# One product in wider superblocks: 1024 and 512 tokens in place of 768, with pairs of weight sets in step

## The chip, the cores and the metric

The kernel runs on one core of a Trainium2 chip. Measured is the device time of one execution in microseconds (us); the median of three runs of the kernel before is 1436.38 us (1436.04 to 1436.53). A core has five engines that run side by side, each in its own order: TensorE (PE; its weight loads stand as PEld), VectorE (DVE), ScalarE (ACT), GpSimd (POOL) and SyncE (SP). DMAs are issued by SP, ACT and POOL and move data between the memory of the chip (HBM) and the core's SBUF. TensorE writes its results into PSUM, eight banks of 512 float32 per partition, which VectorE and ScalarE read.

## The reference

```python
scores = scale * q @ k.T                       # 8 batches, 8 heads, 576 tokens, 64 wide
x = ((scores * Dmat) @ v)                      # decay gamma ** (i - j) for i >= j, as (4608, 512)
h = (x @ w1) * (x @ w2) @ w3                   # 512 -> 1024 -> 1024
x = h @ w_out                                  # (4608, 512)
h = x @ w_in                                   # moe2: 512 -> 2048
g = h * np.clip(h + 3.0, 0.0, 6.0) / 6.0
out = g @ w_out2                               # 2048 -> 512
```

All in float32. The change is about `h = x @ w_in` and what makes g of it.

## The kernel before

Four stages follow each other on TensorE: the weights w3 @ w_out (start to about 60 us), attention and the first expert layer by blocks of 512 tokens (to 730.69 us, line 704), the first product of moe2 (to 1081.57, lines 895 to 924), and its second product (to the end, line 993). Precise products are made of three matmuls, high x high, high x low and low x high (`mm3`, lines 124 to 128), on operands of the type float32r.

The first product of moe2 works on 2 x 2 blocks by a scheme with seven products in place of eight (Strassen's, in Winograd's form). The weights stand in eight *sets* (`wset`), each with seven 256 x 128 combinations; the tokens in *superblocks* with seven *operands* (`xop`), each a combination of token halves and of halves of the 512 inputs, high and low part. A superblock of the kernel before has 2 x 384 = 768 tokens, and there are six. For each superblock and each set, `run_set` (line 771) makes seven products; each is 2 halves (`kk`) x 3 = 6 matmuls of 384 columns, in the order of the operands 0 to 6. They go to four banks: A takes products 0 and 3, B product 1, D products 2 and 5, C products 4 and 6. After product 0 ScalarE copies A into u; U = u + B and V = U + D are made by VectorE; the results are A after product 3, c22 = V + C, c12 = U + D and c21 = U + C after the last accumulation. The seventh product of a set comes after the first one of the next set (`pending`).

Each result goes through `gate` (line 743): ScalarE makes relu(r / 6 + 1/2), VectorE min(that, 1) times the result, and POOL issues the store to `gd` in HBM. Results wait for their store in tiles of `g_tile` (line 736): six of 384 columns and four more in two staging tiles `gw`, in turn. A tile is written again only when its store has landed. In the first set of the first superblock the relu's output takes such a tile as well.

The order of the work is written out by hand: `at(s, f)` puts f before the s-th call of `tick`, and each `mm3` makes one tick. That sets the order on each engine; when an instruction runs is decided by its semaphores. Operands are stored to HBM (`xod`) by the blocks of the stage before (`x2_store`, line 616) and loaded by SP (`load_xop`, line 680) into a ring of eleven places of 1536 columns; at the end of a superblock three places are free beyond the seven in use, and loads of the next operands start as places come free. Sets of weights are loaded once, from 706 us on (`load_set`, line 667); set 3 and later ones at the start of the stage. In the last superblock the places of weights that are done take the operands of the second product (`q_tile`, `q_late`).

Of the kernel before, what the change touches and what calls it, by code (L numbers as in the profile page):

```python
# [26 lines left out]
def retention_moe_kernel(  # L27
# [37 lines left out]
    BLK = 384  # L65
# [3 lines left out]
    NSB = NT // (2 * BLK)  # L69
    NSET = M2 // 2  # L70
    NX = 11
# [8 lines left out]
    xod = dram_p.tile([NSB, 7, 128, 2, 2, BLK], F32, name="xod")  # L80
# [234 lines left out]
    with tc.manual_schedule():  # L315
# [300 lines left out]
        def x2_store(j, kk):  # L616
            c = HB1 * j
            while c < HB1 * j + HB1:
                sb, a = divmod(c, BLK)
                n = min(BLK - a, HB1 * j + HB1 - c)  # L620
                for hl, t in enumerate((x2b["hi"], x2b["lo"])):
                    (nc.sync if j == NB - 1 else nc.scalar).dma_start(
                        out=xod[sb, :, :, kk, hl, a:a + n].rearrange("o p n -> p o n"),
                        in_=t[:, 0:7 * HB1].rearrange("p (o n) -> p o n", o=7)[:, :, c - HB1 * j:c - HB1 * j + n])
                c += n
# [41 lines left out]
        def load_set(n, pool, tag):  # L667
            wset[n] = w = pool.tile([128, 2, 7 * 256], F32R, tag=tag, name="wset")
            if n == 2:
                nc.scalar.copy(out=w[:, 0, 0:1], in_=half)  # L670
            elif n < 2:
                nc.gpsimd.memset(w.bitcast(F32)[:, 0, 0:1], 0.0)
            nc.sync.dma_start(out=w.bitcast(F32), in_=wid[n].rearrange("h p n -> p h n"))

        def ring(q, shape, dtype, name):
            k = q % NX
            pool = xo_p if 5 <= k < 7 else ap["xr" if k < 5 else "xl"]
            return pool.tile(shape, dtype, tag={5: "xh", 6: "xl"}.get(k, f"x{k}"), name=name)

        def load_xop(sb, i):  # L680
            xop[sb, i] = x = ring(7 * sb + i, [128, 2, 2, BLK], F32R, "xop")
            if sb == 0:
                nc.gpsimd.memset(x.bitcast(F32)[:, 0, 0, 0:1], 0.0)
            nc.sync.dma_start(out=x.bitcast(F32), in_=xod[sb, OPS[i]])
# [13 lines left out]
        for i, s in enumerate((20, 26, 32, 38, 44, 4, 52)):  # L698
            at(E0 + s, lambda i=i: load_xop(0, i))
# [14 lines left out]
        g_p = ctx.enter_context(tc.tile_pool(name="gp", bufs=6))  # L714
# [7 lines left out]
        tmp = [x[:, BLK * i:BLK * i + BLK] for x in (stg, stg_hi) for i in range(4)]  # L722
        t_at = {"u": (7,), "U": (5, 6), "V": (4, 3), "r": (0, 1, 2)}
# [9 lines left out]
        g_more = [wf_p.tile([128, 1024], F32, tag="wr", name="gw") for _ in range(2)]  # L733
        g_n = [0]

        def g_tile():
            g_n[0] += 1
            i, k = divmod(g_n[0] % 10 - 6, 2)
            if i < 0 or not g_more:
                return g_p.tile([128, BLK], F32, tag="g", name="g")  # L740
            return g_more[i][:, BLK * k:BLK * k + BLK]

        def gate(src, sb, m, h, keep=True):
            c = {}

            def f0():
                c["r"] = g_tile() if (sb, m % NSET) == (0, 0) else temp("r")
                nc.scalar.activation(out=c["r"], in_=src(), func=ACTF.Relu, bias=half, scale=1.0 / 6.0)

            def f1():  # L750
                c["g"] = src() if keep else g_tile()
# [3 lines left out]
            def f2():  # L755
                p0 = (2 * sb + h) * BLK
                nc.gpsimd.dma_start(out=gd[:, m, p0:p0 + BLK], in_=c["g"])

            for d, f in ((0, f0), (3, f1), (6, f2)):
                at(now[0] + d, f)  # L760

        def prod(sb, n, i, o, ps_, first, stop):
            w, x = wset[n], xop[sb, i]
            for kk in range(2):
                cs = slice(o * 256 + kk * 128, o * 256 + kk * 128 + 128)
                mm3(ps_[:, 0:BLK], w[:, 0, cs], w[:, 1, cs], x[:, kk, 0], x[:, kk, 1], first and kk == 0, stop and kk == 1, skip_group_check=True)
# [4 lines left out]
        def run_set(sb, n):  # L771
            c = {}

            def bank(k):
                c[k] = ps_bank()

            def u_copy():
                c["u"] = temp("u")
                nc.scalar.copy(out=c["u"], in_=c["A"][:, 0:BLK])

            def u2():
                c["U"] = temp("U")
                add(c["U"], c["u"], c["B"][:, 0:BLK])

            def v():
                c["V"] = temp("V")
                add(c["V"], c["U"], c["D"][:, 0:BLK])

            def c_of(k, a, b):
                def f():  # L790
                    c[k] = g_tile()
                    add(c[k], c[a], c[b][:, 0:BLK])
                return f

            bank("A")
            prod(sb, n, 0, 1, c["A"], True, True)
            at(now[0], u_copy)
            if pending:
                pending.pop()()
            bank("B")  # L800
            prod(sb, n, 1, 4, c["B"], True, True)
            at(now[0], u2)
            bank("D")
            prod(sb, n, 2, 3, c["D"], True, True)
            at(now[0], v)
            prod(sb, n, 3, 2, c["A"], False, True)
            gate(lambda: c["A"][:, 0:BLK], sb, n, 0, keep=False)
            bank("C")
# [252 lines left out]
```

## Time and profile before

| | |
|---|---|
| median of 3 runs | 1436.38 us |
| profiled execution | 1436.19 us |
| its span, from the first to the last instruction | 1434.4 us |
| busy: TensorE, weight loads, VectorE, ScalarE, GpSimd | 1428.4, 1241.8, 1019.0, 582.4, 153.1 us |
| first product of moe2 | 730.69 to 1081.57 us |
| HBM read and written | 175.94 and 109.58 MB |

The profiled execution's own time is its span and 1.8 us around it. Busy time of a matmul is modelled, and two that follow each other overlap, so what a matmul costs is read from the starts of its neighbours. The idle time of an engine that isn't the bottleneck costs nothing by itself. In the rows, "<-" behind an instruction stands between what it writes and what it reads; in brackets stands what ended the idle time before it.

### The profile page before, as it was taken

How to read it: one execution, taken by the hardware profiler on the slowest of the kernel's cores; microseconds unless marked ns; L12 is line 12 of the kernel's file. 1: busy time of each engine (PE TensorE's matmuls, PEld its weight loads, DVE VectorE, ACT ScalarE, POOL GpSimd, SP SyncE). 2: the span in 40 equal slices, each digit the busy share in tenths (PEclk: the TensorE clock that was granted, in tenths of full speed). 3: DMA queues.
4: the chain of work that ended last, by engine and by line, in shares of the span. 5: the costliest groups of instructions: out<-in, count | busy, mean ns of one | idle time of the engine just before them, and what ended most of it. 6: DMA issues, size and time to landing. Idle time of an engine off the chain costs nothing.

```text
span 1434.4 us, 27310 instructions
## 1 busy us (share of the span) xinstructions
PE 1428.4 (100%) x11144; PEld 1241.8 (87%) x11144; DVE 1019.0 (71%) x1751; ACT 582.4 (41%) x894; POOL 153.1 (11%) x283
## 2 busy tenths in 40 slices
PE   9999999999999999999999999999999999999999
PEld 4588888888888888888899999999999888888888
DVE  7897566665666656573556666666678889988997
ACT  6583334333434334343333333333344443343343
POOL 1101000000000000000012333223320000000000
PEclk9999999999999999999999999999999999999999
DMA  9843646464656555555799563645699444455541
GB/s 359 310 147 109 224 160 223 143 241 141 211 172 192 191 182 198 170 183 159 274 342 392 231 254 115 265 173 201 220 387 308 133 122 123 138 147 147 144 123 57
DMA packets 187021, 287.29 MB, mean 200 GB/s; under 512 B 9776, under 2 KB 141136, under 8 KB 186896
## 3 DMA queue, kind: packets, MB, share of 16 engines
q1 hardware_dynamic: 107568, 153.11, 31.8%
q0 software_dynamic: 22304, 73.72, 14.1%
q10 hardware_dynamic: 57024, 58.73, 12.2%
q8 instruction: 87, 1.43, 0.4%
q14 instruction: 38, 0.31, 0.1%
HBM read 175.94 MB, written 109.58 MB: 199 GB/s over the span
## 4 chain that ended last, share of the span: by engine, by line
PE 99%; DMA 0%; DVE 0%; ACT 0%; issue 0%
PE pb L983 16%; PE pb L126 13%; PE pb L128 13%; PE pb L127 13%; PE pb L984 8%; PE px L126 5%; PE pa L126 5%; PE pa L127 5%; PE px L128 5%; PE px L127 5%; PE pa L128 5%; PE Wps L487 4%; PE z L209 3%; PE sc L209 2%; DMA orawA<-in_w_out_dram 0%; PE pb L981 0%
## 5 line engine op out<-in xcount | busy, mean ns | idle before, releaser
L983 PE MATMUL pb<-wq,op 128*128 128x512 f32 x1000 | 346.7, 391 | 0.0
L984 PE MATMUL pb<-wq,op 128*128 128x256 f32 x1000 | 280.5, 280 | 0.0
L128 PE MATMUL pb<-xop,wset 128*128 128x384 f32 x672 | 226.1, 336 | 0.0
L127 PE MATMUL pb<-xop,wset 128*128 128x384 f32 x672 | 225.8, 336 | 0.0
L126 PE MATMUL pb<-xop,wset 128*128 128x384 f32 x672 | 225.5, 336 | 0.2 <-issue 0.2
L983 PEld LDWEIGHTS pb<-wq,op 128*128 128x128 f32 x1000 | 187.1, 187 | 40.6
L886 ACT CAST op<-unit 128x1024 fp32r<-128x1024 f32 x126 | 131.3, 1050 | 173.7 <-DVE unit L872 150.9
L984 PEld LDWEIGHTS pb<-wq,op 128*128 128x128 f32 x1000 | 189.4, 189 | 0.0
L131 DVE TENSOR_TENSOR op<-unit,op 128x1024 fp32r<-128x1024 f32 x126 | 154.1, 1223 | 30.3 <-ACT op L886 30.3
L126 PEld LDWEIGHTS pb<-xop,wset 128*128 128x128 f32 x672 | 126.3, 188 | 0.5 <-issue 0.5
L127 PEld LDWEIGHTS pb<-xop,wset 128*128 128x128 f32 x672 | 126.3, 188 | 0.0
L128 PEld LDWEIGHTS pb<-xop,wset 128*128 128x128 f32 x672 | 126.3, 188 | 0.0
L126 PE MATMUL pa<-xh,w1h 128*128 128x512 f32 x288 | 114.1, 396 | 0.0
L126 PE MATMUL px<-abh,Wh 128*128 128x512 f32 x288 | 113.9, 396 | 0.0
L126 PE MATMUL pb<-xh,w2h 128*128 128x512 f32 x288 | 112.4, 390 | 0.0
L127 PE MATMUL pa<-xl,w1h 128*128 128x512 f32 x288 | 112.4, 390 | 0.0
L128 PE MATMUL pa<-xh,w1l 128*128 128x512 f32 x288 | 112.4, 390 | 0.0
L128 PE MATMUL px<-abh,Wl 128*128 128x512 f32 x288 | 112.3, 390 | 0.0
L127 PE MATMUL px<-abl,Wh 128*128 128x512 f32 x288 | 112.3, 390 | 0.0
L127 PE MATMUL pb<-xl,w2h 128*128 128x512 f32 x288 | 112.2, 389 | 0.0
L128 PE MATMUL pb<-xh,w2l 128*128 128x512 f32 x288 | 112.1, 389 | 0.0
L731 DVE TENSOR_TENSOR stghi<-stghi,pb 128x256 f32<-128x256 f32 (+1 forms) x163 | 78.0, 479 | 27.5 <-PE pb L128 26.1
(146 smaller groups left out, 2251.1 us busy)
## 6 DMA issues: line engine op xcount, KB each, us to landing
unit<-gd SPq DMA_DIRECT2D x72, 512.0 KB, 5.2
xop<-xod SPq DMA_DIRECT2D x42, 768.0 KB, 8.4
gd<-g POOLq DMA_DIRECT2D x122, 192.0 KB, 5.0
qk<-in_qk_dram POOLq DMA_DIRECT2D x36, 512.0 KB, 6.1
kv<-in_kv_dram POOLq DMA_DIRECT2D x32, 512.0 KB, 5.1
wset<-wid SPq DMA_DIRECT2D x8, 1792.0 KB, 14.4
wq<-wqd SPq DMA_DIRECT2D x28, 512.0 KB, 8.9
gd<-gw POOLq DMA_DIRECT2D x70, 192.0 KB, 3.8
```

What stands on the lines that cost most here:

```text
L126: nc.tensor.matmul(out=out_ap, lhsT=sh, rhs=mh, start=first, stop=False, **kw)
L127: nc.tensor.matmul(out=out_ap, lhsT=sh, rhs=ml, start=False, stop=False, **kw)
L128: nc.tensor.matmul(out=out_ap, lhsT=sl, rhs=mh, start=False, stop=last, **kw)
L131: eng.tensor_tensor(out=out_ap, in0=x, in1=y, op=ALU.subtract)
L209: nc.tensor.matmul(out=out_ap, lhsT=lhsT, rhs=rhs, start=True, stop=True, skip_group_check=True)
L487: nc.tensor.matmul(out=ps, lhsT=w3f[:, n // 4 % 8, n % 4 * 128:n % 4 * 128 + 128], rhs=wo[:, j, :], start=j == 0, stop=j == KF - 1)
L731: nc.vector.tensor_tensor(out=out_ap, in0=a, in1=b, op=ALU.add)
L886: nc.scalar.copy(out=op_tiles(7 * b + p)[0], in_=src())
L983: nc.tensor.matmul(out=c[k], lhsT=h[:, ts], rhs=w, start=first and kt == 0, stop=False, skip_group_check=True)
L984: nc.tensor.matmul(out=c[k][:, 0:256], lhsT=l[:, ts], rhs=w[:, 0:256], start=False, stop=kt == 7, skip_group_check=True)
```

## The change

Superblocks become 4 of 1024 tokens and, as the second one, one of 512 (`SBS`: first block of 512 tokens, and how many). Their operands have 4 x 512 or 4 x 256 columns and nine places of 2048 columns instead of eleven of 1536 (`SLOTS` says which operand lies where). The first two sets of every superblock, and the last two except in the last superblock, run in step: product 0 of both, product 1 of both, and so on (`run_sets`), on all eight banks. The second of such a pair takes its u and V from `g_tile`. `g_tile` has three tiles of 512 columns, four halves of the staging tiles, and at the end of the last superblock a 512-column rest of each weight set that is done. Constants and staging go to the right end of SBUF, so that operands lie lower. A weight set of the late ones is loaded by three DMAs instead of one. Operand 6 of the first superblock is loaded at the start of the stage; before, all seven were loaded while the last block of the stage before was in work.

```diff
-    BLK = 384
+    BLK = 512
-    NSB = NT // (2 * BLK)
+    SBS = ((0, 2), (2, 1), (3, 2), (5, 2), (7, 2))
+    NSB = len(SBS)
+    WID = [n * HB1 for _, n in SBS]
...
-    const_p = ctx.enter_context(tc.tile_pool(name="const", bufs=1))
+    const_p = ctx.enter_context(tc.tile_pool(name="const", bufs=1, side="right"))
-    wf_p = ctx.enter_context(tc.tile_pool(name="wf", bufs=2))
+    wf_p = ctx.enter_context(tc.tile_pool(name="wf", bufs=2, side="right"))
...
+        SLOTS = (tuple(range(7)), (7, 7, 8, 8, 0, 0, 1), (2, 3, 4, 5, 6, 7, 8), (0, 1, 2, 3, 4, 5, 6), (7, 8, 0, 1, 2, 3, 4))
...
         def load_xop(sb, i):
-            xop[sb, i] = x = ring(7 * sb + i, [128, 2, 2, BLK], F32R, "xop")
+            k, w = SLOTS[sb][i], 4 * WID[sb]
+            if w == 2048 or (sb, k) not in share:
+                share[sb, k] = [place(k, "xop"), 0]
...
-        for i, s in enumerate((20, 26, 32, 38, 44, 4, 52)):
+        for i, s in enumerate((4, 52, 20, 26, 32, 38, 104)):
             at(E0 + s, lambda i=i: load_xop(0, i))
...
-        g_p = ctx.enter_context(tc.tile_pool(name="gp", bufs=6))
+        g_p = ctx.enter_context(tc.tile_pool(name="gp", bufs=3))
...
         def g_tile():
             g_n[0] += 1
-            i, k = divmod(g_n[0] % 10 - 6, 2)
-            if i < 0 or not g_more:
-                return g_p.tile([128, BLK], F32, tag="g", name="g")
-            return g_more[i][:, BLK * k:BLK * k + BLK]
+            i = g_n[0] % (3 + len(g_more)) - 3
+            return g_more[i] if i >= 0 else g_p.tile([128, BLK], F32, tag="g", name="g")
...
+            def own(k):
+                return (g_tile() if second and k in "uV" else temp(k))[:, 0:w]
...
+        def run_sets(groups, after=()):
+            for i in range(6):
+                for g in groups:
+                    g[i]()
+                if i == 0:
+                    while pending:
+                        pending.pop(0)()
+                if i < len(after):
+                    after[i]()
+            pending.extend(g[6] for g in groups)
...
+        EARLY = ({4: (0, 1), 5: (2, 3)}, {0: (0, 1), 2: (2,), 3: (3,), 4: (4,)}, {2: (0,), 4: (1,)}, {2: (0,), 4: (1,)})
+        LATE = (((4,), (5,), (6,)), ((), (5,), (), (6,)), tuple((i,) for i in range(2, 7)), tuple((i,) for i in range(2, 7)))
...
-                run_set(sb, n)
+                if k in (1, 7) and (k == 1 or sb < NSB - 1):
+                    continue
+                if k == 0:
+                    run_sets([set_steps(sb, n), set_steps(sb, SETS[1], True)])
+                elif k == 6 and sb < NSB - 1:
+                    run_sets([set_steps(sb, n), set_steps(sb, SETS[7], True)],
+                             [lambda v=v: [load_xop(sb + 1, i) for i in v] for v in LATE[sb]])
+                else:
+                    run_sets([set_steps(sb, n)])
```

On TensorE the stage starts before with the products of one set; `pb_7480` is its bank A, `pb_7489` its bank B, and the `wset` number is the set:

```order
L126 MATMUL pb_7480<-xop_7088,wset_7310 128x384
L127 MATMUL pb_7480<-xop_7088,wset_7310 128x384
L128 MATMUL pb_7480<-xop_7088,wset_7310 128x384
...
L126 MATMUL pb_7489<-xop_7122,wset_7310 128x384
L127 MATMUL pb_7489<-xop_7122,wset_7310 128x384
L128 MATMUL pb_7489<-xop_7122,wset_7310 128x384
```

and now, with bank A of the first set (`pb_7472`), bank A of the second (`pb_7487`) and bank B of the first (`pb_7500`):

```order
L127 MATMUL pb_7472<-xop_6988,wset_7299 128x512
L128 MATMUL pb_7472<-xop_6988,wset_7299 128x512
L129 MATMUL pb_7472<-xop_6988,wset_7299 128x512
...
L127 MATMUL pb_7487<-xop_6988,wset_7336 128x512
L128 MATMUL pb_7487<-xop_6988,wset_7336 128x512
L129 MATMUL pb_7487<-xop_6988,wset_7336 128x512
...
L127 MATMUL pb_7500<-xop_7248,wset_7299 128x512
L128 MATMUL pb_7500<-xop_7248,wset_7299 128x512
L129 MATMUL pb_7500<-xop_7248,wset_7299 128x512
```

The second product on the same operand is the other set's, and every product has 512 columns.

On VectorE, at the same place, the first set's results and the start of the second set stand so before (`g` and `gw` are tiles that wait for a store; DMASW is a semaphore of POOL's stores):

```order
L731 TENSOR_TENSOR g_7525<-stg_71,pb_7514 128x384 [waits DVE_49,PE_49]
L752 SCALAR_TENSOR_TENSOR g_7532<-g_7517,pb_7480 128x384 [waits Activation_49]
L731 TENSOR_TENSOR g_7538<-stghi_72,pb_7499 128x384 [waits PE_49]
L752 SCALAR_TENSOR_TENSOR g_7525<-g_7527,g_7525 128x384 [waits Activation_49]
L752 SCALAR_TENSOR_TENSOR g_7538<-gw_7478,g_7538 128x384 [waits Activation_49]
L731 TENSOR_TENSOR gw_7478<-stghi_72,pb_7514 128x384 [waits PE_49]
L731 TENSOR_TENSOR stghi_72<-stghi_72,pb_7559 128x384 [waits PE_49,Activation_49]
```

and now the last results of the first pair, from the first set's c12 on, so:

```order
L748 TENSOR_TENSOR g_7588<-stghi_76,pb_7517 128x512 [waits DVE_49,PE_49]
L768 SCALAR_TENSOR_TENSOR g_7577<-stg_75,g_7577 128x512 [waits Activation_49]
L748 TENSOR_TENSOR gw_7470<-stghi_76,pb_7528 128x512 [waits DMASW2_49,PE_49]
L768 SCALAR_TENSOR_TENSOR g_7588<-gw_7470,g_7588 128x512 [waits Activation_49]
L768 SCALAR_TENSOR_TENSOR gw_7470<-stg_75,gw_7470 128x512 [waits Activation_49]
L748 TENSOR_TENSOR gw_7471<-stghi_76,pb_7556 128x512 [waits DMASW4_49,PE_49]
L748 TENSOR_TENSOR g_7634<-stghi_76,pb_7565 128x512 [waits DMASW3_49,PE_49]
L768 SCALAR_TENSOR_TENSOR gw_7471<-gw_7471 128x512 [waits Activation_49]
L748 TENSOR_TENSOR stghi_76<-stghi_76,pb_7633 128x512 [waits PE_49]
L768 SCALAR_TENSOR_TENSOR g_7634<-stg_75,g_7634 128x512 [waits Activation_49]
L748 TENSOR_TENSOR stg_75<-stghi_76,pb_7644 128x512 [waits DVE_49,PE_49]
```

Three results (the second set's c12, and c21 of both) now wait for a store of this pair before they are written; U and V of the next set stand behind them.

## Rows read from the trace of the kernel before

**Rows 1.** The page: busy us (share) of engines; granted clock in 40 slices.
```profile
PE 1428.4 (100%) x11144; PEld 1241.8 (87%) x11144; DVE 1019.0 (71%) x1751; ACT 582.4 (41%) x894; POOL 153.1 (11%) x283
PEclk9999999999999999999999999999999999999999
```
**Rows 2.** TensorE's three waits, first and last: who for whom, us, times, longest.
```profile
PE zero L477 <- POOL Wh L475: 2.1, 1, 2.1
...
PE pb L126 <- issue: 0.2, 1, 0.2
```
**Rows 3.** The stage, wset's instructions: us, busy (count) of PE, PEld, ACT, POOL, clock...
```profile
730.69:1081.57 350.88, 350.69 (x2016) 350.25 (x2015) 0.00 (x0) 0.00 (x0) 1.00 0.68 257
```
**Rows 4.** TensorE's timeline (start us, us) at 512, 384, 256 columns; one line by source.
```profile
699.63 0.39 PE L127 MATMUL pa<-xl,w1h 128*128 128x512 f32 x1
...
701.90 0.39 PE L128 MATMUL pb<-xh,w2l 128*128 128x512 f32 x1
...
850.49 0.34 PE L126 MATMUL pb<-xop,wset 128*128 128x384 f32 x1
...
851.39 0.33 PE L128 MATMUL pb<-xop,wset 128*128 128x384 f32 x1
...
852.95 0.33 PE L128 MATMUL pb<-xop,wset 128*128 128x384 f32 x1
...
1429.79 1.48 PE L981 MATMUL pb<-wq,op 128*128 128x256 f32 x11
...
L981 PE MATMUL pb<-wq,op x24: 279/283/284, 1428.2 to 1431.0; 128*128 128x256 f32 x24
```
**Rows 5.** Timeline at the stage's start, TensorE and ScalarE.
```profile
733.63 0.34 PE L128 MATMUL pb<-xop,wset 128*128 128x384 f32 x1
734.16 0.41 PE L126 MATMUL pb<-xop,wset 128*128 128x384 f32 x1 [0.19 <-issue]
734.41 0.34 PE L127 MATMUL pb<-xop,wset 128*128 128x384 f32 x1
...
733.59 0.47 ACT L779 COPY stghi<-pb 128x384 f32<-128x384 f32 x1
```
**Rows 6.** DMAs from 730 to 790; landings of weights (735 to 745) and x2l stores.
```profile
DMA packets 6778, 22.28 MB, mean 371 GB/s; under 512 B 672, under 2 KB 3390, under 8 KB 6774
...
L673 SPq DMA_DIRECT2D wset<-wid x5: 359/560/1353, 735.4 to 742.6; - x5
DMA to landing us min/median/max: 11.7/19.4/30.3
...
L622 SPq DMA_DIRECT2D xod<-x2l x2: 359/360/360, 733.7 to 735.0; - x2
DMA to landing us min/median/max: 4.1/5.3/6.5
```
**Rows 7.** Stores of g: 865 to 895, 743 to 790, 737 to 742.5.
```profile
DMA to landing us min/median/max: 2.1/2.1/2.6
...
DMA to landing us min/median/max: 2.3/6.4/8.9
...
DMA to landing us min/median/max: 8.2/8.4/9.2
```
**Rows 8.** By line (busy us, mean ns): VectorE, ScalarE; VectorE's timeline at 384.
```profile
L550 DVE TENSOR_TENSOR ab<-a,pb 128x512 f32<-128x512 f32 x27 | 18.5, 685 | 19.3 <-PE pb L128 19.3
L731 DVE TENSOR_TENSOR stghi<-stghi,pb 128x256 f32<-128x256 f32 x78 | 32.7, 419 | 1.2
...
L748 ACT ACTIVATE stg<-g,half 128x384 f32<-128x384 f32 x72 | 44.5, 617 | 62.0 <-DVE g L731 62.0
...
736.52 0.56 DVE L731 TENSOR_TENSOR g<-stg,pb 128x384 f32<-128x384 f32 x1 [0.46 <-PE pb L128]
736.99 0.55 DVE L752 SCALAR_TENSOR_TENSOR g<-g,pb 128x384 f32<-128x384 f32 x1
```
**Rows 9.** One of VectorE's two waits for stores from 740 to 1030.
```profile
DVE g L731 <- DMA gd<-g: 1.5, 1, 1.5
```

More of the change, by code (lines that the diff above doesn't have):

```diff
@@ L616, in x2_store @@
         def x2_store(j, kk):
[L617 to L625, printed above, removed]
+            sb = next(i for i, (b0, n) in enumerate(SBS) if b0 <= j < b0 + n)
+            a = HB1 * (j - SBS[sb][0])
+            for hl, t in enumerate((x2b["hi"], x2b["lo"])):
+                (nc.sync if j == NB - 1 else nc.scalar).dma_start(
+                    out=xod[sb][:, :, kk, hl, a:a + HB1].rearrange("o p n -> p o n"),
+                    in_=t[:, 0:7 * HB1].rearrange("p (o n) -> p o n", o=7))
         open_ab()
@@ new lines, in load_set, with set_part, place @@
+            for t, h, p, q in parts:
+                c = 0 if p else 1792 * h
+                nc.sync.dma_start(out=t.bitcast(F32)[:, c:c + q - p], in_=wid[n, h, :, p:q])
+        def set_part(n, h, c):
+            w, t = wset[n]
+            c += 1792 * h
+            return w[:, c:c + 128] if t is w or c < 3072 else t[:, c - 3072:c - 2944]
+        SLOTS = (tuple(range(7)), (7, 7, 8, 8, 0, 0, 1), (2, 3, 4, 5, 6, 7, 8), (0, 1, 2, 3, 4, 5, 6), (7, 8, 0, 1, 2, 3, 4))
+        share = {}
+        def place(k, name):
+            pool = xo_p if k < 2 else ap["xr" if k < 6 else "xl"]
+            return pool.tile([128, 2048], F32R, tag=("xh", "xl")[k] if k < 2 else f"x{k}", name=name)
@@ L772, in run_set @@
             c = {}
+            w = WID[sb]
             def bank(k):
-                c[k] = ps_bank()
+                c[k] = ps_bank()[:, 0:w]
+            def own(k):
+                return (g_tile() if second and k in "uV" else temp(k))[:, 0:w]
             def u_copy():
-                c["u"] = temp("u")
-                nc.scalar.copy(out=c["u"], in_=c["A"][:, 0:BLK])
+                c["u"] = own("u")
+                nc.scalar.copy(out=c["u"], in_=c["A"])
             def u2():
-                c["U"] = temp("U")
@@ L795, in run_set @@
[L795 to L808, printed above, removed]
@@ L809, in run_set, with s0 @@
-            prod(sb, n, 4, 5, c["C"], True, True)
-            at(now[0], c_of("c22", "V", "C"))
-            gate(lambda: c["c22"], sb, n + NSET, 1)
-            prod(sb, n, 5, 6, c["D"], False, True)
-            at(now[0], c_of("c12", "U", "D"))
-            gate(lambda: c["c12"], sb, n, 1)
-            def end():
+                    c[k] = g_tile()[:, 0:w]
+                    add(c[k], c[a], c[b])
+                return f
+            def s0():
+                bank("A")
+                prod(sb, n, 0, 1, c["A"], True, True)
+                at(now[0], u_copy)
@@ new lines, in s1, with s2, s3, s4 @@
+            def s1():
+                bank("B")
+                prod(sb, n, 1, 4, c["B"], True, True)
+                at(now[0], u2)
+            def s2():
+                bank("D")
+                prod(sb, n, 2, 3, c["D"], True, True)
+                at(now[0], v)
+            def s3():
+                prod(sb, n, 3, 2, c["A"], False, True)
+                gate(lambda: c["A"], sb, n, 0, keep=False)
+            def s4():
+                bank("C")
+                prod(sb, n, 4, 5, c["C"], True, True)
+                at(now[0], c_of("c22", "V", "C"))
+                gate(lambda: c["c22"], sb, n + NSET, 1)
@@ L817, in end, with s5, s6 @@
+            def s5():
+                prod(sb, n, 5, 6, c["D"], False, True)
+                at(now[0], c_of("c12", "U", "D"))
+                gate(lambda: c["c12"], sb, n, 1)
+            def s6():
                 prod(sb, n, 6, 0, c["C"], False, True)
@@ L844, in f32_unit @@
             if k not in un:
-                un[k] = ring(k, [128, 1024], F32, "unit")
+                p = {9: 5, 10: 5, 0: 6, 1: 6, 2: 7, 3: 7, 4: 8, 7: 8, 8: 2}[k]
+                if p not in at_unit:
+                    at_unit[p] = [place(p, "unit").bitcast(F32), 0]
+                x, a = at_unit[p]
+                at_unit[p][1] = 1024
+                un[k] = x[:, a:a + 1024]
             return un[k]
```

83 lines of the change are left out of this document (41 added, 42 removed).

## The prediction

> **What bounds the kernel now.** I read the page first, then the stages, then the spacing of matmuls, and only then the queues. TensorE is busy for 1428.4 of the 1434.4 us at a granted clock that stays at full speed in all 40 slices [rows 1], and in the whole program it waits three times, 2.9 us in all [rows 2]. No other engine comes near: VectorE has 71%. So time can only come from the spacing of the matmuls, or go into new waits of TensorE. The changed stage is the stretch from 730.69 to 1081.57 us: 350.88 us for 2016 matmuls, 174.0 ns each [rows 3].
>
> What does one matmul cost as a function of its columns? Its modelled duration (0.34 us at 384 columns) overlaps the next one, so the reader is to look at the starts. At 512 columns ten starts span 699.63 to 701.90, 227 ns each; at 384, nine spacings span 851.39 to 852.95, 173.3 ns each; at 256, a merged row of 11 gives (1.48 - 0.28) / 10 = 120 ns, 0.28 being the duration of a single one [rows 4]. Between 256 and 512 that is 107 ns for 256 columns, 0.417 ns per column (2.4 GHz), and at no columns about 13.3 ns are left. 384/2.4 + 13.3 = 173.3 is what the third row shows. Thus, in these rows, every matmul pays 13.3 ns beside its columns, whatever its width. There are as many weight loads as matmuls [rows 1], so loads keep up with that pace at 256 columns, too.
>
> **The change part by part.** *Fewer, wider matmuls.* A set of weights takes 7 products x 2 halves x 3 = 42 matmuls in each superblock. Before: 6 superblocks x 8 sets x 42 = 2016 of 384 columns. After: 4 x 8 x 42 = 1344 of 512, and 8 x 42 = 336 of 256. Columns are the same (774,144). By the law: 2016 x 0.17333 = 349.44 us; after it 1344 x 0.22667 + 336 x 0.120 = 304.64 + 40.32 = 344.96. The term is -4.48 us, 336 x 13.33 ns. No wait hides it: TensorE is the bound of this stage throughout.
>
> The Trainium skill, "TensorE: Matmul & The Clock Gate" (Part 1, on 56 ns against 53.3), has a rule that speaks against this change: back to back, a warm matmul takes N/2.4 plus about 2.5 ns. By it the term would be 336 x 2.5 ns = 0.84 us. The rows here, with float32 operands, show 13.3 and not 2.5 at each of three widths, so the sum goes by the rows.
>
> *What the law leaves over in this stage:* 350.88 - 349.44 = 1.44 us. Of it 0.43 is one hiccup: matmuls at 733.63 and 734.16 start 0.53 us apart and the next one 0.25, where 0.173 is due: +0.35, +0.08 [rows 5]. The matmul at 734.16 accumulates into the bank that a copy on ScalarE still reads (733.59 + 0.47 = 734.06); this copy stands behind the casts of the last block's x2l. In step, the accumulation into the first bank comes as seventh product and not as fourth, 6 x 1.36 = 8.16 us after the first product instead of 3.1 us. The copy is done by then: -0.43. The other 1.01 us are small irregularities, some 20 ns per set: from 850.49 to 851.39 five spacings take 0.90 us where the law gives 0.87 [rows 4]. They recur at the same places, where operands change. The operands' places in SBUF all move, so I bound this from 0.84 us after (40 sets at 21 ns) to nothing, and take the middle, 0.4: -0.6.
>
> *Products of two sets in step.* Order of matmuls alone; each operand now serves two sets in a row, and a bank is read twice as late. The eight banks are all taken by a pair. A bank is needed again at the earliest one whole set later, 9.5 us at 512 columns, and its readers take 0.7 us each. Cost nothing; the cover is these 9.5 us.
>
> *Operands.* The last of the seven operands of the first superblock is now loaded when the stage begins, on SP's queue behind the two stores of x2l and ahead of the weights of sets 3 to 7. It is needed for the seventh product of the first pair, after 13 products: 730.69 + 13 x 1.36 = 748.4. Before, the first of five weight loads stood in this place: issued at 735.4, 1792 KB, landed 11.7 us later, at 747.1 [rows 6]. 1024 KB can't take longer in the same place, so at least 1.3 us are spare. The weights behind it come about 1024/1792 x 5.7 = 3.3 us later (5.7: first weights' 747.1 less the x2l stores' last landing, 735.0 + 6.5 = 741.5, [rows 6]), and set 3 is wanted at 730.69 + 20 x 1.36 = 757.9. Nothing. At later borders operands come in as the steps of the last pair free their places, from 13.6 us ahead of the border on; five loads of 1 MB are 14 us at the 371 GB/s that full queues moved [rows 6], and each is used 21 us or more after its place came free. Nothing, too.
>
> *Places for g.* Results waiting to be stored have seven places of 512 columns, before ten of 384, and pairs write more of them at once. So a write may now wait for a landing: the order shows VectorE's sixth result of the first pair, and then the seventh and eighth, behind such stores. A landing takes 2.1 us with no loads about (865 to 895) and 2.3, 6.4, 8.9 (least, median, most) while weights come in (743 to 790); the four stores before these took 8.2, 8.4, 9.2 [rows 7]. I follow the tightest place, in us from the stage's start, with 1.36 per product. VectorE's operation lasts 0.69 us at 512 columns, and one starts 0.08 before the other ends (736.52 + 0.56 against 736.99) [rows 8]. Product C of the pair's first set ends at 12.24, its sum is at 13.1, the relu on ScalarE (0.62 at 384 columns, [rows 8]) at 13.9, the gate's product at 15.1, its store starts at 15.2. The pair's seventh result wants this place. It is followed by the eighth, two gates' products with a relu between, u and v: 4.0 us, six operations at 0.6 and 0.4 for ScalarE. TensorE accumulates over the bank that v reads after 19 products, at 25.84. So TensorE waits when 15.2 + landing + 4.0 > 25.84, with landings over 6.6 us: with the median 0, with 9.2 us 2.6 us. This store comes early in the traffic, so I take 7.4, midway between the median and the 8.4 of the first four: 0.8; ends 0 and 2.6. Later sets of 9.5 us cover the median.
>
> In the superblock of 512 tokens a set takes 42 x 0.12 = 5.04 us. VectorE's nine operations at 0.42 (256 columns, [rows 8]) are 3.8 us: it keeps up. Its stores have about 7 us to land (below). At 2.1 to 6.4: nothing.
>
> *Edits with one answer:* whole stores of x2 in place of pieces, the new addresses of constants and staging, the places of the second product's units. All lie beside TensorE's work; the second product's weights come into places of sets that are done, and a set before the end is now 9.5 us and not 7.3. Nothing; bounds 0 and +1.5 us, if a change of operand costs 12 ns in each of the 126 products there (20 ns per set of 7 operands in the stage above is the nearest row).
>
> **Sum.** Against the profiled execution (1436.19, of which 1434.4 span): -4.48 - 0.43 - 0.6 + 0.8 = -4.7, so 1431.5. The median of the runs is 0.2 above the profiled one: 1431.7.
>
> **Rivals.** (A) *Landings of stores at their worst.* For: DMAs are busy without a break there, and before, too, VectorE waited for a place twice, 1.5 us at longest [rows 9]. Against: of 25 landings from 743 on half took 6.4 or less. TensorE would lose 2.6 and not 0.8 here, and about 1 at the border to the 512-token superblock, where VectorE has about 6 us for a landing: 1431.7 + 1.8 + 1 = 1434.5.
>
> (B) *The fixed cost belongs not to the matmul but to its columns.* Were the 227 ns at 512 all in the columns, 384 would take 170 and 256 113.5, and the 336 matmuls fewer would be worth nothing: 1436.4 - 0.4 - 0.6 + 0.8 = 1436.2. Against it stand 173.3 and 120 [rows 4]. The skill's 2.5 ns, above, lies near this case: 0.84 less.
>
> (C) *Slower: the 512-token superblock runs at the pace of its stores.* A set there writes four places in 5.04 us, and seven places turn over in 8.8 us. Sum, relu and product before the store take 1.7 us, so a landing may last 7.1. All 7 MB of the next superblock's operands are due in these 40 us. Were landings 9.2 us throughout, a place would be taken for 10.9 us, a set would last 6.2 us and eight of them 9.5 us longer: 1441.2. It decides from landings over 7.1 us for most of the 40 us. Against: DMAs move 371 GB/s when full [rows 6], so 7 MB take 19 us, and about half of it is ahead of this superblock.
>
> **How the numbers follow.** The measurement can tell about 0.2% (2.9 us) from no change. Forecast 68%, its own range 1430.4 (no irregularities left, no wait) to 1433.2 (all of them, and most of the wait's upper end); A 18%; B 4%; C 7%; the rest, 3%, is a late operand that I don't see. A lies astride the limit of 1433.5: half faster, half the same; a little of the forecast comes out nearer than 2.9 us, if what I cost at nothing in the last stage costs its 1.5. Faster 0.76, same 0.15, slower 0.09. The range leaves out B, C and the upper part of A: 1430.2 to 1434.2.
>
> **What would show it.** In the profile after: 1344 matmuls of 512 and 336 of 256 columns at the same line, the stage at 345 to 347 us (350.88 before), spacings of 227 and 120 ns; no start 0.5 us late three us into the stage; VectorE waiting for stores of g at about 747 to 754 us, TensorE hardly. It would be wrong if 256-column matmuls were spaced by much over 120 ns, if TensorE's waits for VectorE or a load summed to over 3 us, or if the last stage grew.

## The result, and the profile after

The changed kernel takes 1451.59 us (median of four runs, 1449.41 to 1453.16), the kernel before beside it 1436.45 (1436.04 to 1436.59): ratio 1.0105, 95% interval 1.0087 to 1.0122. The forecast was 1431.7 and faster; the kernel is 15 us slower. The profiled execution took 1453.16 us, its span is 17.0 us longer than that of before; it was the slowest of the four.

The page after, busy time and TensorE's busy share in 40 slices, beside [rows 1]: 336 matmuls fewer, and a slice (the 30th) in which TensorE is no longer full.

```profile
PE 1435.5 (99%) x10808; PEld 1185.5 (82%) x10808; DVE 1010.5 (70%) x1679; ACT 574.8 (40%) x854; POOL 135.8 (9%) x251
PE   9999999999999999999999999999979999999999
```

TensorE's waits after, beside [rows 2]; who for whom, us, times, longest:

```profile
PE pb L127 <- DVE stg L748: 8.8, 4, 6.9
...
PE pb L127 <- DVE gw L748: 1.3, 1, 1.3
```

The changed stage after, beside [rows 3] (wset's instructions; stretch, length, busy and count of PE, PEld, ACT, POOL, clock, DMA share, GB/s):

```profile
730.71:1092.47 361.76, 351.71 (x1680) 293.55 (x1679) 0.00 (x0) 0.00 (x0) 0.99 0.68 254
```

The last stage by all engines (PE, PEld, DVE, ACT, POOL, clock): before and, below, after. The third and fourth rows are the same 100 us of each.

```profile
1081.57:1434.40 352.83, 349.69 (x2025) 308.89 (x2024) 312.31 (x415) 138.37 (x163) 1.72 (x4) 1.00 0.48 140
...
1200.00:1300.00 100.00, 100.00 (x579) 88.30 (x578) 89.70 (x119) 40.00 (x47) 0.00 (x0) 1.00 0.50 141
```

```profile
1092.47:1451.40 358.93, 355.83 (x2025) 309.53 (x2023) 312.55 (x414) 138.95 (x162) 1.63 (x3) 1.00 0.45 130
...
1200.00:1300.00 100.00, 100.00 (x569) 86.97 (x568) 88.49 (x117) 39.06 (x45) 0.00 (x0) 1.00 0.47 135
```

So the 17.0 us are 361.76 - 350.88 = +10.9 in the changed stage and 358.93 - 352.83 = +6.1 in the last, where TensorE's instructions are those of before but for the places of their operands: as many matmuls, at a full clock, always busy, but 569 in 100 us and not 579. A product of this stage is eight pairs of matmuls, 512 columns and 256. Before, each takes 2773 ns, 346.7 a pair, and that is the prediction's law (226.7 + 120); after, they take 2803, 2830 and 2833 in turn. I call the first the short pace and the others, 2803 to 2834, the long one.

Where are the 10.9 us? In TensorE's timeline I took each start, subtracted the one before it, and then the law of the prediction. Late starts stand out: 0.4 us at 756, 1.45 at 818, 1.06 at 823, 0.9 at 1070, and one of 7.1 at 1081. First the two at 818 and 823, with VectorE's wait for a store ahead of them; then TensorE and VectorE around the last one:

```profile
819.65 0.38 PE L127 MATMUL pb<-xop,wset 128*128 128x256 f32 x1 [1.29 <-DVE gw L748]
...
824.50 0.39 PE L127 MATMUL pb<-xop,wset 128*128 128x256 f32 x1 [0.90 <-DVE stg L748]
...
818.84 0.42 DVE L768 SCALAR_TENSOR_TENSOR gw<-stg,pb 128x256 f32<-128x256 f32 x1 [2.39 <-DMA gd<-gw]
```

```profile
1080.78 0.40 PE L129 MATMUL pb<-xop,wset 128*128 128x512 f32 x1
1088.11 0.79 PE L127 MATMUL pb<-xop,wset 128*128 128x512 f32 x1 [6.93 <-DVE stg L748]
1088.70 0.63 PE L128 MATMUL pb<-xop,wset 128*128 128x512 f32 x1
1089.12 0.63 PE L129 MATMUL pb<-xop,wset 128*128 128x512 f32 x1
...
1091.56 0.39 PE L129 MATMUL pb<-xop,wset 128*128 128x512 f32 x1
...
1075.46 0.68 DVE L768 SCALAR_TENSOR_TENSOR gt<-stg,gt 128x512 f32<-128x512 f32 x1
...
1085.22 0.69 DVE L748 TENSOR_TENSOR gt<-stghi,pb 128x512 f32<-128x512 f32 x1 [8.14 <-DMA gd<-gt]
...
1087.37 0.68 DVE L748 TENSOR_TENSOR stg<-stghi,pb 128x512 f32<-128x512 f32 x1
```

Read the last one from below. TensorE waits for `V` (1087.37), which lets it accumulate over bank D. VectorE could not make it earlier since it stood 8.14 us at 1085.22: it wanted to write c21 of the set into a place whose store had not landed. That place was written last at 1075.46, by the same set's c22. A row of the DMA view from 1074 to 1086 gives that store's landing (KB, us), and the clock behind the wait stands in a stretch of all engines:

```profile
gd<-gt POOLq DMA_DIRECT2D x1, 256.0 KB, 8.5
...
1088.10:1091.40 3.30, 3.29 (x8) 2.62 (x9) 2.61 (x4) 1.52 (x2) 0.84 (x2) 0.50 0.30 107
```

After 7 us at rest TensorE runs at 0.50 (1.2 GHz) for 3.3 us: eight spacings take 3.45 us (1088.11 to 1091.56) and not 1.81, another 1.6 us. The sum: -4.48 and -0.43 as forecast, +13.0 in waits (7.1 + 1.6 + 1.45 + 1.06 + 0.9 + 0.4, and 0.5 in the starts right behind them, 0.1 each), and 2.8 that are left. These are not in waits: products of 512 columns take mostly 0, 13, 21 or 30 ns too long, a given operand nearly always the same amount, 3.8 us in all (1.0 before); those of 256 columns, whose operands all stand at the left end, keep to 120 ns a matmul.

### The profile page after: what moved, and what is told of

The parts are those of the page before. It is cut to its first block, busy times and chain, and to the rows that moved or that the text cites. A ratio compares the mean times of both kernels' runs of the same rounds, so it can differ in the third digit from the quotient of the medians.

```text
span 1451.4 us, 26347 instructions
## 1 busy us (share of the span) xinstructions
PE 1435.5 (99%) x10808; PEld 1185.5 (82%) x10808; DVE 1010.5 (70%) x1679; ACT 574.8 (40%) x854; POOL 135.8 (9%) x251
## 5 line engine op out<-in xcount | busy, mean ns | idle before, releaser
L1036 PE MATMUL pb<-wq,op 128*128 128x512 f32 x1000 | 352.8, 398 | 0.0
L127 PE MATMUL pb<-xop,wset 128*128 128x512 f32 (+1 forms) x560 | 209.5, 374 | 10.0 <-DVE stg L748 8.8
L129 PE MATMUL pb<-xop,wset 128*128 128x512 f32 (+1 forms) x560 | 207.8, 371 | 0.0
L128 PE MATMUL pb<-xop,wset 128*128 128x512 f32 (+1 forms) x560 | 206.8, 369 | 0.0
L127 PEld LDWEIGHTS pb<-xop,wset 128*128 128x128 f32 x560 | 106.0, 189 | 29.5 <-DVE stg L748 10.3
L129 PEld LDWEIGHTS pb<-xop,wset 128*128 128x128 f32 x560 | 105.9, 189 | 19.7
L128 PEld LDWEIGHTS pb<-xop,wset 128*128 128x128 f32 x560 | 106.0, 189 | 18.8
L917 DVE TENSOR_TENSOR unit<-unit 128x1024 f32<-128x1024 f32 x72 | 87.9, 1221 | 0.6
```

The costliest lines, as they stand in the source:

```text
L127: nc.tensor.matmul(out=out_ap, lhsT=sh, rhs=mh, start=first, stop=False, **kw)
L128: nc.tensor.matmul(out=out_ap, lhsT=sh, rhs=ml, start=False, stop=False, **kw)
L129: nc.tensor.matmul(out=out_ap, lhsT=sl, rhs=mh, start=False, stop=last, **kw)
L917: nc.vector.tensor_tensor(out=f32_unit(o), in0=t[0], in1=t[1], op=f)
L1036: nc.tensor.matmul(out=c[k], lhsT=h[:, ts], rhs=w, start=first and kt == 0, stop=False, skip_group_check=True)
```

## The experiments

Times are medians; the kernel before, run beside them, stayed at 1436.3 to 1436.4.

**1. The place of the pools alone, undone and done.** e1, the changed kernel with `side="right"` taken from two pools; e2, the kernel before with it, which is shown ("..." stands for lines left out):

```diff
-const_p = ctx.enter_context(tc.tile_pool(name="const", bufs=1))
+const_p = ctx.enter_context(tc.tile_pool(name="const", bufs=1, side="right"))
...
-wf_p = ctx.enter_context(tc.tile_pool(name="wf", bufs=2))
+wf_p = ctx.enter_context(tc.tile_pool(name="wf", bufs=2, side="right"))
```

> The changed kernel with one part undone: the pools of the constants (and staging) and of the second product's small weights go back to the left end of SBUF, so that every operand of the last two stages moves up by about 15 KB. Instructions and their order stay as they are. Theory P (the place of the operands in SBUF sets the spacing): a product of the last stage falls from 2803 to 2834 ns back to 2773, the stage from 359 to 353 us, some of the 3 ns per matmul of 512 columns in the changed stage goes too, and the time is 1443 to 1446 us. Rival S (the stream of instructions sets it: program length, fetching, queues): the products stay at 2803 and 2834 ns and the time at 1449 to 1453 us. The wait of 7 us at the end of the changed stage stays by both.

> The kernel before with this one part of the change alone: the same two pools at the right end of SBUF, so that operands move down by about 15 KB. Theory P: the last stage grows from 353 to about 359 us, products from 2773 to 2803 to 2834 ns, and the time is 1440 to 1443 us. Rival S: 1436.4 us, products at 2773 ns.

e1: 1450.27 us, unlike P: its last stage stays long (569 matmuls in 100 us). The wait ahead of it, which by both was to stay at 7 us, is 3.6 us here. e2: 1442.54 us, as P has it; instructions, order and waits are those of before. Its two stages:

```profile
730.89:1081.78 350.89, 350.70 (x2016) 350.25 (x2015) 0.00 (x0) 0.00 (x0) 1.00 0.68 257
...
1081.78:1440.80 359.02, 355.82 (x2025) 309.54 (x2024) 312.42 (x415) 139.69 (x163) 1.71 (x4) 1.00 0.47 138
```

So addresses alone can bring the whole 6.1 us of the last stage; the rival S falls for the kernel before. But the way back doesn't undo it in the changed kernel, so the region isn't all of it.

**2. The place used longest ago (e3).**

```diff
...
-g_n[0] += 1
-i = g_n[0] % (3 + len(g_more)) - 3
-return g_more[i] if i >= 0 else g_p.tile([128, BLK], F32, tag="g", name="g")
+g_free.append(g_free.pop(0))          # three of g_p and g_more; new places go to the front
+return g_free[-1] if g_free[-1] is not None else g_p.tile([128, BLK], F32, tag="g", name="g")
```

> The changed kernel, with one rule exchanged: a result to be stored takes the place that was used longest ago, from a list, instead of the place that a running number modulo the number of places gives (which, when a place is added, hands out the one just used). As many places as before. Theory G (the 7.1 us wait at 1080 us comes from a result written into the place that the result before it has just left, whose store takes 8.5 us to land): each place is now written again a set of 9.5 us later, the wait shrinks to 0 to 2 us, the stretch at half clock behind it (1.6 us) goes, and the time falls by 6.5 to 8.7 us, to 1443 to 1445 us. Rival L (the landing itself is the bound, because loads are ahead of all stores there; whichever place it is, a write waits for one): the wait stays over 4 us and the time over 1447 us.

1443.08 us, -8.5. TensorE's waits in this stage are now:

```profile
PE pb L127 <- DVE stg L748: 1.2, 2, 0.9
PE pb L127 <- DVE gw L748: 1.1, 1, 1.1
```

G holds: no start is late after 824 us (the 0.9 at 1070 went, too), and the half clock is gone; between the two traces the stage is 361.76 - 351.99 = 9.8 us shorter. What failed was the modulo, which handed out again the place just used when `g_more` grew from one to two; the stores there land after 5.1 and 5.9 us (medians of two kinds, 1064 to 1078), which a turn of a whole set covers.

**3. Both edits (e4).**

> The changed kernel with the oldest place used first and with constants and small weights back at the left end (both edits of the two runs before this one together). Last-stage operands for products 1 to 4 then stand at the same addresses as in the kernel before, and no stall precedes the last stage. Theory H (two rhythms: a stream of back-to-back pairs of matmuls keeps the rhythm it entered with; the run with the left end alone was slow because of the 3.75 us stall ahead of it): products at 2773 ns, the last stage 6.2 us shorter than with the oldest place alone, 1443.1 - 6.2 = 1436.9 us. Rival U (the units and later weights, which stand elsewhere than before the change, or the stream, set the rhythm): products stay at 2820 to 2830 ns, 1443 us.

1443.31 us, the last stage still at the long pace (x568 in 100 us). H, as I put it, falls: no stall goes before, and the first four products have their operands where they were in the kernel before.

**4. Alignment in the kernel before (e5, e6).** 32 bytes left free, in e5 behind the first constant, in e6 at the left end with the pools at the right:

```diff
+const_p.tile([128, 8], F32, name="pad")     # e5
+wab_p.tile([128, 8], F32, name="pad")       # e6
```

> The kernel before with 32 bytes left free behind the first constant, so that all operands of the last two stages move from 32 to 0 modulo 64 bytes and nothing else moves by more. Theory M (the alignment of the operands' rows within 64 bytes sets the rhythm: 32 in the kernel before, 0 in the changed one): the last stage grows by about 6 us to 1442.5 us, products at 2803 to 2834 ns. Rival R (the region of SBUF, or which operands share one): 1436.3 us, products at 2773 ns.

> The kernel before with the two pools at the right end, and 32 bytes left free at the left end, so that operands stand about 15 KB lower than before but again at 32 modulo 64 bytes (except the two small-weight places, which stay at the right at 0 modulo 64). Theory M: two of three products (with stationary operands in the low places) return to 2773 ns, the time to 1436.3 to 1438.5 us. Rival R: 1442.5 us as without the free bytes.

e5: 1435.91, last stage short (x578). e6: 1442.15, long (x568). M falls: 0 or 32 modulo 64 doesn't set the pace. Two things in e6 were new. Its first product is short and the second long, though only the first has operands of different remainder, and no start between them is late:

```profile
1081.20:1083.97 2.77, 2.77 (x17) 2.43 (x17) 2.34 (x4) 1.47 (x4) 0.63 (x2) 1.00 1.05 406
1083.97:1086.81 2.84, 2.84 (x19) 2.47 (x18) 2.43 (x4) 2.16 (x3) 1.08 (x2) 1.00 1.02 394
```

And in e5 the small excesses of the first product's stage (16, 12, -5, -3 ns a product before) became 7, 8, 0, -1: they follow the difference between operands at the left end and at the right (64 bytes modulo 256 before, 32 in e5).

**5. Halved places (e7).** In the superblock of 512 tokens two results share a place:

```diff
+if w in g_rest:
+    return g_rest.pop(w)
 ...
+if w < BLK:
+    g_rest[w] = x[:, w:BLK]
+return x[:, 0:w]
```

> The changed kernel with the oldest place used first, and in the superblock of 512 tokens two results of 256 columns share a place of 512 (seven places hold fourteen results there). Theory G (too few places for results whose stores have not landed): the starts that come 1.25 and 1.05 us late at 818 and 823 us go, and the time falls by 2.3 us from 1443.1 to 1440.8. Rival L (stores land too late there, whatever the places; VectorE stands behind the store of the pair before the border, at 809 to 812 us): 0 to 0.7 us are gained, 1442.4 to 1443.1 us.

1441.62 us: both late starts are gone (-2.3), but one of 0.85 us came up at 1058, where the last superblock has three places. It is the only wait of TensorE for VectorE that the profile still lists:

```profile
PE pb L127 <- DVE stg L748: 0.7, 1, 0.7
```

**6. All operands of one remainder (e8, e9, e10), and mixed (e11).** e8: 1856 bytes behind the last right-hand place; e9: 64 bytes at the left end; e10: these in e2; e11: e9 with the places 2, 3 and 4 moved by 64 bytes.

```diff
+n = 464 if k == 5 else 0                    # e8 (pools left): tile [128, 2048 + n], used [:, 0:2048]
...
+wab_p.tile([128, 16], F32, name="pad")      # e9 to e11
...
+n = 16 if k == 5 else 0                     # e11: tile [128, 2048 + n], used [:, n:]
```

> The changed kernel with the oldest place first, halved places in the small superblock, both pools back at the left end, and 1856 bytes left free above the right-hand operands of the first product, so that every operand of TensorE in the last two stages stands at 160 modulo 2048 bytes (in the runs before, left-hand places were at 160 and right-hand ones at 2016). Theory A (matmuls whose moving operands change between places of different remainder lose 13 to 30 ns a product, and the pace so entered is kept until something ends it, so that the last stage, entered from a right-hand operand, stays slow for all its 126 products): the 4.4 us spread over the 512-column matmuls fall to under 1 us, products of the last stage take 2773 ns, the time is 1441.6 - 3.5 to 4.4 - 6.2 = 1431 to 1432 us. Rival R (the region of SBUF or the stream of instructions): the pattern by operand stays, 1441 to 1443 us.

> The changed kernel with the oldest place first and halved places, both pools at the right end as in the change, and 64 bytes left free at the left end: left-hand operands go from 1152 to 1216 (192 modulo 256), right-hand ones and the small weights' places stand at 192 modulo 256 already, but differ by 256 modulo 512. Theory A with a period of 256 bytes or less: as in the run with all aligned, 1431 to 1432 us. Theory A with a longer period (512 to 2048 bytes): the excess changes its size, but does not vanish, 1435 to 1443 us. Rival R: 1441.6 us, as without the free bytes.

> The kernel before with the two pools at the right end (1442.5 us alone) and 64 bytes left free at the left end, which puts all operands of the last two stages at 192 modulo 256. Theory A with a period of 256 bytes or less: the last stage returns from 355.4 to 349.3 us, and the transitions in the first product's stage go (1 us): 1435.3 to 1436.3 us. Rival R: 1442.5 us.

> The kernel with 64 bytes free at the left end, but three of the first product's nine operand places (used for the last three products of the last superblock, and in no product of the last stage) moved by 64 bytes, so that the last stage is entered from operands of another remainder while all its own agree. Theory A, with its pace kept once entered: the last stage is slow from end to end (products at 2820 to 2834 ns, 6 us) and the first product's stage loses 2 to 4 us at changes of operands: 1439 to 1442 us. Rival N (no memory: only the addresses of the products at hand count): the last stage is fast (2773 ns), 1433 to 1436 us.

1438.86, 1438.96, 1435.41 and 1442.86 us. The stage of the first product in e7 and in e9, and the same 40 us in e9 and e11 (wset's instructions):

```profile
730.72:1080.92 350.20, 349.39 (x1680) 292.34 (x1679) 0.00 (x0) 0.00 (x0) 1.00 0.69 259
```

```profile
730.84:1077.83 346.99, 345.88 (x1680) 292.32 (x1679) 0.00 (x0) 0.00 (x0) 1.00 0.70 261
...
865.00:905.00 40.00, 40.00 (x178) 33.13 (x177) 0.00 (x0) 0.00 (x0) 1.00 0.30 115
```

```profile
865.00:905.00 40.00, 40.00 (x175) 32.58 (x174) 0.00 (x0) 0.00 (x0) 1.00 0.31 119
```

A holds for this stage in that remainders set the excess: with one remainder modulo 256 that of 512-column products is zero wherever no wait is near, and 3.7 us are back (3.2 in the stage, since its waits are 0.4 us longer than in e7). That it is paid at a change from place to place falls: in e11 each product from a moved place takes 40 ns more, all along a run of such products. In e10, the kernel before with both pools at the right, the excess is gone, too, and the last stage is short again:

```profile
730.96:1080.83 349.87, 349.70 (x2016) 349.26 (x2015) 0.00 (x0) 0.00 (x0) 1.00 0.68 257
...
1080.83:1433.70 352.87, 349.69 (x2025) 308.49 (x2024) 312.22 (x415) 138.51 (x163) 1.72 (x4) 1.00 0.48 140
```

But e8 and e9 missed by 7 us: their last stage stays long, with all operands agreeing and no wait at its entry. e9:

```profile
1200.00:1300.00 100.00, 100.00 (x568) 86.68 (x567) 87.79 (x117) 40.03 (x46) 0.00 (x0) 1.00 0.48 135
```

e11 is long, too, and so tells nothing apart.

**7. A pause (e14), in e10.** The first operand's halves are made at the end of the last set:

```diff
-prep(0, 0, now[0] + 4, 4)        # in the seventh set
+prep(0, 0, s + 11, 2)            # in the eighth
```

> The kernel before with both pools at the right end and 64 bytes free (1435.4 us, products of the last stage at 2773 ns), with one edit: the two halves of the last stage's first operand are made so late that TensorE pauses for about 1 us at the stage's first pair. Addresses and the order of matmuls stay. Theory K (the pace is kept from the entry; a stream that starts from a pause falls into the long one): all 126 products at 2820 to 2834 ns, the time 1435.4 + 1 + 6.6 = 1443 us. Rival N (no memory): the pause alone, 1436 to 1436.8 us.

Of ten executions eight took 1441.97 to 1442.44 us, two 1436.21 and 1436.60. The trace of a long one shows the switch. Starts of the second, the sixth, the seventh and the eleventh product of the last stage, and the pause within the sixth:

```profile
1083.75 0.39 PE L983 MATMUL pb<-wq,op 128*128 128x512 f32 x1
...
1094.84 0.39 PE L983 MATMUL pb<-wq,op 128*128 128x512 f32 x1
1095.23 0.39 PE L984 MATMUL pb<-wq,op 128*128 128x256 f32 x1
1095.45 0.39 PE L983 MATMUL pb<-wq,op 128*128 128x512 f32 x1
...
1097.92 0.40 PE L983 MATMUL pb<-wq,op 128*128 128x512 f32 x1
...
1109.23 0.40 PE L983 MATMUL pb<-wq,op 128*128 128x512 f32 x1
```

Four products take 11.09 us (2773 ns each) up to 1094.84. There two starts come 0.26 us late together, and from then on four take 11.31 (2828 ns), to the end of the stage. The same places, instructions and clock: K holds in its core. The stream of pairs has two paces, here 346.7 and 353.3 ns, and kept each of them for as long as nothing disturbed it. The long products of e14 have the same three lengths in turn (2831, 2819, 2830 ns) as those of e4, e8 and e9, so theirs is the same pace. My "a pause brings the long one" is not a rule: the pause at the stage's very start (0.2 us) left it short. Of 94 timed executions of the kernel before, one took 1443.20 us and all others 1436.0 to 1436.8; there is no trace of that one.

**8. Other orders of the last stage's matmuls (e12, e13, e15, e16).** e12: e9 with each product as eight matmuls of 512 columns, then eight of 256. e13: two places more in the sixth set, too. e15: e13 with this order in the first product alone. e16: e13 in twos (512, 512, 256, 256).

```diff
-for kt in range(8):              # 512 and 256 columns in turn
+for i in range(16):
...
+    kt = i % 8                   # e12, e13: 512 columns where i < 8
+    kt = i // 4 * 2 + i % 2      # e16: 512 columns where i % 4 < 2
...
-g_free[:] = [x for x in g_free if x is None]                              # sixth set
+g_free[:] = [x for x in g_free if not any(x is y for y in g_more)]        # e13: seventh
```

> The kernel with 64 bytes free at the left end (1439.0 us, all operands agree modulo 256, last stage still at 2820 to 2834 ns a product), with the matmuls of each product of the last stage in another order: first the eight of 512 columns, then the eight of 256, instead of eight pairs of 512 and 256. Theory K (the alternation 512, 256 has two lasting paces, and which one it has is kept from the entry; runs of one width have only the short pace, as the stage of the first product shows): products at 2773 ns, the last stage 349.3 us instead of 356, 1432.3 us. Rival D (something else in the last stage costs 6.7 ns a pair, say VectorE's and ScalarE's or the DMAs' use of SBUF): 1438 to 1440 us.

> As the run before it in this call, and two places for results more in the sixth set of the last superblock: the two small-weight places are given up a set later, and the high and low parts of the last stage's first operand, which go there, are made a set later. Theory G (too few places): the late start of 1.2 us at 1054 us goes, 1431.0 us, if theory K holds too. Rival L (landings): it moves to the seventh set, 1432 us or more.

> The best kernel so far (1433.3 us: places, alignment, and each product of the last stage as eight matmuls of 512 columns, then eight of 256, which costs 20 ns at each product's changes of width, 2.5 us), with the eight-and-eight order in the first product of the last stage alone; the other 125 are pairs again, entered from a run of 256 columns. Theory K leaves open which pace such an entry gives: with the short one 349.4 us for the stage and 1430.9 us in all; with the long one 356 us and 1437.6. Rival to K (the alternation itself is slow in this kernel, whatever its entry): 1437.6 us, too, but then the pace is long from the first pair on in every execution; a mixture of both times in the executions, or a change of pace inside one, speaks for K.

> The same kernel with each product of the last stage in groups of two: two matmuls of 512 columns, two of 256, and so on. Theory K (it is the alternation 512, 256 that has two paces): either another pair of paces, or the 20 ns at a change of width paid four times a product, 80 ns and 10 us at most, 1433.3 + 0 to 7.5 us; no gain over eight and eight is expected, and a product under 2794 ns would speak against a cost of the change of width itself.

1434.64, 1433.32, 1437.61 and 1432.76 us. The first product's stage of e13 and TensorE's one wait in it, then 100 us of the last stage in e13, e15 and e16:

```profile
730.73:1076.29 345.56, 345.34 (x1680) 292.31 (x1679) 0.00 (x0) 0.00 (x0) 1.00 0.70 263
...
PE pb L128 <- DVE stg L749: 0.2, 1, 0.2
...
1200.00:1300.00 100.00, 100.00 (x576) 88.02 (x575) 89.07 (x119) 39.52 (x46) 0.00 (x0) 1.00 0.49 138
```

```profile
1200.00:1300.00 100.00, 100.00 (x568) 86.78 (x568) 88.36 (x117) 39.16 (x45) 0.00 (x0) 1.00 0.48 135
```

```profile
1200.00:1300.00 100.00, 100.00 (x576) 87.32 (x575) 89.33 (x119) 39.61 (x46) 0.00 (x0) 1.00 0.49 138
```

Taking the strict alternation away brings back most of the 6.7 us in the same kernel, at the same places, so the rival D falls. The other orders cost 20 ns a product (2793) by eights and 14 (2787) by twos. Four times as many changes of width cost less, so the 20 ns don't belong to a change of width; what they do belong to, no run shows. In e13 the late start of 1.1 us that e12 has at 1055 is gone and none took its place: G, not L. e15 is long in all ten executions by their times, and in its trace from its second product on: a run of 256 columns is no way into the short pace, and K and its rival stay apart only by e14. e16 beats both kernels: 0.9975 of the time before (0.9965 to 0.9985).

## Why the prediction was wrong

The gain came as forecast. What failed are costs that the prediction put at nothing or bounded too tightly: 13.0 us of waits, 2.8 of irregularities, and 6.1 in a stage that it took for untouched.

**Right: the law and the -4.48.** With places enough and one remainder the stage takes 345.56 us (e13), inside the 345 to 347 that the prediction named; the law alone gives 344.96. 256-column matmuls are 120 ns apart. That is 350.88 - 345.56 = 5.3 us, of which the remainder alone makes 1.0 (e10's stage takes 349.87 with the old blocks); 4.3 are the wider blocks. Rival B falls. So does, for these float32r matmuls, the extra 2.5 ns of the Trainium skill, "TensorE: Matmul & The Clock Gate" (Part 1): 13.3 stand in its place.

**Right: the late copy** at 733.6 [rows 5]: no late start before 756.

**The size: waits in the first superblock.** 0.8 forecast, 0.4 measured, at 756.

**Failed: "Places for g ... Later sets of 9.5 us cover the median."** I followed the first pair's tightest place and took the rest by a median, with seven places. At the end of the last superblock there are three and one or two of another kind, the rule of numbers hands out the place just used, and landings are 8.5 us under the second product's loads. That made 0.9 us at 1070, then 7.1 and, by the clock, 1.6 more (e3: -8.5 by the medians). The row that warned of it was there, [rows 7] with 8.2 to 9.2 us under load; I did not set it against the turn of this place, which is wanted 1.6 us after it was written (1075.46, and 1085.22 - 8.14 = 1077.08).

**Failed: "In the superblock of 512 tokens ... Nothing."** 2.5 us at its beginning, where results of a 1024-token pair hold the places (e7: -2.3). Rival C had the mechanism, but as a pace of eight sets; it was two starts.

**Failed: "Edits with one answer ... Nothing; bounds 0 and +1.5 us."** The bound took 12 ns for each of 126 products. It was 6.1 us, 49 ns each, since it isn't paid at a change of operand: it is some 6 ns in every pair of matmuls, a pace. "It would be wrong ... if the last stage grew" was the right thing to look at.

**Failed: the irregularities, -0.6.** They grew by 2.8 us where I had bounded them by what was there. They depend on the difference of two places in bytes, and all places were moved. e9 shows that they can be zero.

The Trainium skill, "SBUF — State Buffer" (Who interferes with whom), says that TensorE reads moving operand and weights by two independent ports and never waits on anyone. It names no effect of addresses there; the runs show one: 64 bytes left free change the spacing of TensorE's matmuls (e7 and e9, 3.2 us; e2 and e10, 6.2 us at equal instructions). In e11 the moved places 2, 3 and 4 agree with one another, and each of their products loses 40 ns, also behind another of them; what they differ from is the weights. Which of the two is held up, no run shows.

Open is what decides between the two paces at the entry. By their places the operands of the last stage have one remainder modulo 256 in the kernel before, e5 and e10, and these are short; they have two in e2 (64 bytes apart, as in the change) and e6 (32), and these are long. So in the kernel before a second remainder was enough for the long pace. It isn't needed: e14 fell into it without, and in the changed kernel all entries tried (from right-hand operands, with one remainder as in e1, e4, e8 and e9, from a run of 256 columns) gave it; the kernel before enters from 384 columns. What at the changed kernel's entry does so, no run shows.

## What to carry to other kernels

Before a stage is widened, count the places for results at its last sets, not at its first, and set the turn of the very place that is handed out next against the slowest landing. Where a change moves pools, compare the operands' addresses modulo 256 bytes and the pace of stages whose code is the same: a full, busy TensorE can lose 2% without a wait. A row of before that looks constant (346.7 ns a pair), and even agrees with the law, may be one of two paces.

## What the runs showed of the hardware that was not expected

- Matmuls of 512 columns whose operands differ by 64 bytes modulo 256 take up to 40 ns more per six (e11), none more at equal remainder (e9).
- Weights and matmuls of 512 and 256 columns in turn run at 346.7 ns a pair or at about 353, and a disturbance of 0.26 us can switch them for the remaining 340 us (e14).
- After 7 us of rest the granted clock was 0.50 (1.2 GHz) for 3.3 us; in e1, after 3.6 us of rest, it was 0.50 for 5.2 us.
